# Moving the low halves of seven x tiles 128 bytes further on in SBUF: an attention and two MLPs on one Trainium2 core

## The chip, the core and the metric

The kernel runs on one core of one Trainium2 chip. The metric is the device time of one execution in microseconds, measured from outside the core's first and last instruction. A profiled execution has a time of its own, a span (first to last instruction) and a trace of every engine.

## What is computed

A causal block attention is followed by two MLPs, all in float32:

```python
scores = scale * np.matmul(q, k.transpose(0, 1, 3, 2))       # q, k, v: 4 x 8 x 576 x 64
scores = np.where(block_i >= block_j, scores, -1e9)          # blocks of 64
attn = softmax(scores)
x = (attn @ v) as 2304 x 512
h = x @ w_in;  x = (h * np.cos(h)) @ w_out                   # d_model 512, d_ff 2048
h = x @ w2_in; x = (np.maximum(h, 0) ** 2) @ w2_out
```

## The kernel before

**Parts and halves.** Each float32 operand of a large product is split into a high half (rounded to float32r) and a low half (the rest). A product is then three matmuls, written by `mm3` (L903): weights high with x high, weights high with x low, weights low with x high. In a matmul the `lhsT` operand is loaded into the array as weights by an instruction of its own, and the `rhs` operand, here x, streams through. Each matmul of the program reloads its weights, so while one matmul streams x, the weights of the next are being loaded.

**Stages.** In the first part (to about 405 us of the span) attention runs on all engines, interleaved with half of the first MLP; nothing of it is touched by the change. From there to the end, three stages run (L1537 on, `R.phase` 5 to 7): the other half of the first MLP, the first half of the second MLP, and its second half. Each stage takes the tokens in five chunks (`ROUNDS`): four of 512 tokens, one of 256. For each chunk there are two `quad` calls (`two` for the chunk of 256), c = 0 and c = 1. A `quad` (L1366) is a Strassen-Winograd product of 2 by 2 blocks: seven products, each of one of seven weight forms with one of seven x forms. One product (L1345) is 12 matmuls of 128 x 128 weights with 256 columns: two column halves m, two row halves k, three matmuls of `mm3`. All are recorded at L548 and named `h<-x,w` in the profile; there are 2304. Products onto `y` (the second matrix of each MLP) run between and among them.

**The order** is set by a list scheduler in the file (`Recorder`), which works on costs of its own and knows no addresses. Each engine then executes its instructions in that order.

**Where the operands lie.** The seven x forms are tiles `x0` to `x6` (`x_tile`, L1299) of [128, 2, 2, 256] float32r: per partition 2048 bytes of high half, then 2048 bytes of low half. They are written by `x_parts` (L1302), and in the second stage also copied to DRAM (`xp_d<-x`); the third stage loads them from there (`x<-xp_d`, `kept_parts`, L1316). The weight forms of c = 0 lie in the pool `wo`, those of c = 1 in the pool `wa` (`factors`, L773), each [128, 2, 512] with the low half 2048 bytes behind the high one. In the built program the starts of these tiles within a partition, modulo 512 bytes, are:

| tiles | start modulo 512 |
|---|---|
| x0 to x6, high and low halves alike | 320 |
| weights of c = 0 (pool `wo`), high and low | 384 |
| weights of c = 1 (pool `wa`), high and low | 256 |
| g tiles (second operand of the y products of the first two stages) | 64 |

All steps from one k, m or half to the next are multiples of 512 bytes. This text calls *distance* the start of the streamed operand less the start of the weights that are loaded meanwhile (the next matmul's), modulo 512 bytes. In a run of products of one `quad` it is the same at every matmul: 448 for c = 0, 64 for c = 1.

Of the kernel before, what the change touches and what calls it, by code (L numbers as in the profile page):

```python
# [2 lines left out]

# [8 lines left out]
F32R = mybir.dt.float32r  # L12
# [6 lines left out]
PSUM = bass.MemoryType.PSUM  # L19
# [37 lines left out]
class View:  # L57
    def __init__(self, vt, chain, ix, halves):
        self.vt, self.chain, self.ix, self.halves = vt, chain, ix, halves
# [34 lines left out]


class VTile(View):
    def __init__(self, pool, shape, dtype, tag, bufs, whole=False):
        self.pool, self.shape, self.dtype, self.tag, self.bufs = pool, shape, dtype, tag, bufs
        self.whole = whole
        n = int(np.prod(shape[1:]))  # L100
        self.grain = 32 if n >= 32 else 1
        self.full = (1 << (2 * (n // self.grain + 1))) - 1
        self.real = None
        self.users = []
        self.bank = self.banks = self.before = None
        super().__init__(self, [], np.arange(n).reshape(shape[1:]), 3)

    def alloc(self):
        if self.real is None:
            tag = self.tag if self.bank is None else f"bank{self.bank}"  # L110
            self.real = self.pool().tile(self.shape, self.dtype, tag=tag, name=self.tag, bufs=self.bufs)


class Banks:
# [30 lines left out]
class Recorder:  # L145
# [20 lines left out]
        self.kind = None  # L166
        self.phase = 0

    def tile(self, pool, shape, dtype, tag, bufs=1, whole=False):
        return VTile(pool, shape, dtype, tag, bufs, whole)  # L170

    @contextmanager
    def of(self, kind):
# [199 lines left out]
def f(v):  # L373
    return v.bitcast(F32)


def real(v):
    return v.ap() if isinstance(v, View) else v
# [3 lines left out]
def kernel(  # L382
# [25 lines left out]
    R = Recorder()  # L408


    def of(kind):
        def wrap(fn):
            def run(*args, **kw):
                with R.of(kind):
                    return fn(*args, **kw)

            return run

        return wrap
# [40 lines left out]
    def hi_part(hi, x):  # L460
        n = hi.size
        flexible(
            "hi",
            {
                "POOL": (
                    "POOL", n * 0.836 + 160,
                    lambda: nc.gpsimd.tensor_scalar(real(hi), real(x), 1.0, 1.0, op0=ALU.mult, op1=ALU.mult),  # L467
                ),
                "DVE": (
                    "DVE", n / 1.92 + 68, lambda: nc.vector.tensor_scalar(real(hi), real(x), 1.0, None, op0=ALU.mult), 2,  # L470
                ),
                "ACT": ("ACT", n / 1.2 + 92, lambda: nc.scalar.activation(real(hi), real(x), ACTF.Copy)),  # L472
            },
            [hi], [x],
        )

    def lo_part(lo, x, hi):
        n = lo.size
        if psum(x):
            return tt(lo, x, f(hi), ALU.subtract)  # L480
        flexible(
            "lo",
            {
                "POOL": (
                    "POOL", n * 2.1 + 350,
                    lambda: nc.gpsimd.tensor_tensor(real(lo), real(x), real(f(hi)), op=ALU.subtract), 1,
                ),
                "DVE": (
                    "DVE", n / 0.96 + 68,
                    lambda: nc.vector.tensor_tensor(real(lo), real(x), real(f(hi)), op=ALU.subtract), 1,  # L490
                ),
            },
            [lo], [x, hi],
        )
# [76 lines left out]
    def dma(out, in_, size, service=None):  # L571
        R.op(
            "DMA", max(400.0, size / 360.0), lambda: nc.sync.dma_start(out=real(out), in_=real(in_)), [out], [in_],
            lat=1250,
        ).service = size / 420.0 if service is None else service
# [5 lines left out]
    class Pool:  # L581


        def __init__(self, name, **kw):
            self.name, self.kw, self.pool, self.after, self.stack = name, kw, None, (), None
# [18 lines left out]
    def later(names, **kw):  # L604
        return [Pool(n, **kw) for n in names]
# [32 lines left out]
    xs_p, tmp = opened(s1, "xs1", "tmp1")  # L638
    (sb,) = opened(att, "att", side="right")

    def T(pool, shape, dtype, tag, bufs=1):
        return R.tile(pool, shape, dtype, tag, bufs, whole=pool.kw.get("space") == PSUM)

    x_d = T(dram, [KD, 128, NT], F32, "x_d")
    y1_d = T(dram, [KD, 128, NT], F32, "y1_d")
    y_d = T(dram, [KD, 128, NT], F32, "y_d")


# [27 lines left out]
    for i in range(2):  # L676
# [3 lines left out]
        whole = T(sb, [128, 128], F32, f"whole{i}")  # L680
# [585 lines left out]
    for group, steps in WORK:  # L1266
# [6 lines left out]
        if group in ((0, 2), (1, 1)):  # L1273
            c = group[0]
            left_weights(w1_in, 2 + c, wi_d[c])
        if group in ((1, 2), (2, 1)):
            c = group[0] - 1
            staged_weights(row_chunks(w1_out, 2 + c, 3 + c), wo_d[c:c + 1])
        if group == (3, 1):
            wo_p, x3_p = later(("wo", "x3"), side="right")  # L1280
# [9 lines left out]
    def raw_rows(src, c0, n):  # L1290
# [5 lines left out]
            raw.append(t)  # L1296
        return raw

    def x_tile(j):  # L1299
        return T(x3_p, [128, 2, 2, 256], F32R, f"x{j}")  # L1300

    def x_parts(forms, keep):  # L1302

        ops = {}
        for j, x in forms:
            t = x_tile(j)
            hi, lo = t[:, 0], t[:, 1]
            hi_part(hi, x)
            lo_part(lo, x, hi)
            if keep is not None:  # L1310
                dma(keep[j], f(t).rearrange("p j k c -> p (j k c)"), 524288)
            ops[j] = hi, lo
        return ops

    @of("forms")
    def kept_parts(keep, which):  # L1316

        ops = {}
        for j in which:
            t = x_tile(j)  # L1320
            dma(f(t).rearrange("p j k c -> p (j k c)"), keep[j], 524288)
            ops[j] = t[:, 0], t[:, 1]
        return ops

    @of("forms")
    def load_plain(src, c0, keep=None):

        x1, x2 = raw_rows(src, c0, 256)
        d = T(tmp3, [128, 2, 256], F32, "t0")
        add(d, x2, x1, ALU.subtract)  # L1330
        return x_parts(((0, x1), (1, x2), (4, d)), keep)

    @of("forms")
    def load_quarters(src, c0, keep=None):

        raw = raw_rows(src, c0, 512)
        b11, b12, b21, b22 = [t[:, :, o:o + 256] for t in raw for o in (0, 256)]
        t1, t2, t3, t4 = [T(tmp3, [128, 2, 256], F32, f"t{i}") for i in range(4)]
        add(t1, b12, b11, ALU.subtract)
        add(t2, b22, t1, ALU.subtract)  # L1340
        add(t3, b22, b12, ALU.subtract)
        add(t4, b21, t2, ALU.subtract)
        return x_parts(enumerate((b11, b21, b22, t4, t1, t2, t3)), keep)
# [193 lines left out]
    for stage in range(3):  # L1537
# [4 lines left out]
        for turn_, i in enumerate(ROUNDS[stage]):  # L1542
# [3 lines left out]
            if stage < 2:  # L1546
                xs = (load_quarters if i < 4 else load_plain)(src, c0, xp_d[i] if stage and turn_ < 4 else None)
                g = new_g()
            else:
                if turn_:  # L1550
                    xs = kept_parts(xp_d[i], FIRST if i < 4 else (0, 1, 4))
                g = g_forms()
# [27 lines left out]
            if stage < 2 and 0 < turn_ < 3:  # L1580
                c = 2 * stage + turn_ - 1
# [61 lines left out]
```

## Time and profile before

| what | value |
|---|---|
| median of 3 runs | 973.34 us (973.02 to 973.65) |
| time of the profiled execution | 974.84 us |
| its span | 973.0 us |
| mean granted TensorE clock | 0.994 of full speed |
| instructions | 19283 |
| TensorE busy (PE) | 98% of the span, 6996 matmuls |
| VectorE, ScalarE, GpSimd busy | 73%, 62%, 21% |
| HBM traffic | 189 GB/s over the span |

PE stands for TensorE's matmuls, PEld for its weight loads, which overlap them; DVE is VectorE, ACT ScalarE, POOL GpSimd, SP the queue that issues the transfers. Matmuls are pipelined: one lasts longer than the time to the start of the next. The time that a matmul costs is therefore read as the length of a stretch divided by the matmuls in it, called *pitch* below, and not as the mean duration of one.

### The profile page before, as it was taken

The page shows a single profiled execution, that of the slowest core. Times are in us where ns is not written, and L with a number is a line of the kernel's source. Part 1 is how long each engine was busy: PE and PEld are TensorE (multiplying, and loading weights), DVE is VectorE, ACT ScalarE, POOL GpSimd, SP SyncE. Part 2 cuts the span into 40 slices and gives each one's busy share as a digit, 9 for nine tenths or more (in the row PEclk, how much of TensorE's full clock was granted, in tenths as well). Part 3 has the DMA queues.
Part 4 walks back from the last instruction along what each step waited for, and adds up shares of the span by engine and source line. Part 5 has one row for each costly group of instructions (what it writes and reads, how often), then busy time and mean ns, then how long its engine had stood idle before and what let it go on. Part 6 is the DMA issues. An engine that isn't in the chain of part 4 may idle for free.

```text
span 973.0 us, 19283 instructions
## 1 busy us (share of the span) xinstructions
PE 951.8 (98%) x6996; PEld 856.1 (88%) x6996; DVE 713.8 (73%) x1581; ACT 602.3 (62%) x1285; POOL 208.3 (21%) x313
## 2 busy tenths in 40 slices
PE   7979999999999999999999999999999999999998
PEld 5757987889898989999989889998898899999998
DVE  5898667687877455588879797987885737659565
ACT  5787588785889575484758476767564433324222
POOL 3554243447687781000000000000000000000000
PEclk8999999999999999999999999999999999999999
DMA  6755233355656347563355899796947779535321
GB/s 184 192 150 124 67 85 84 105 153 182 176 174 206 109 134 263 200 254 93 109 173 181 317 360 327 268 352 215 358 139 240 245 256 416 194 104 195 96 73 60
DMA packets 155150, 185.29 MB, mean 190 GB/s; under 512 B 71728, under 2 KB 119856, under 8 KB 155056
## 3 DMA queue, kind: packets, MB, share of 16 engines
q1 hardware_dynamic: 155056, 184.07, 57.5%
q8 instruction: 55, 0.90, 0.4%
q14 instruction: 39, 0.32, 0.1%
HBM read 114.29 MB, written 69.73 MB: 189 GB/s over the span
## 4 chain that ended last, share of the span: by engine, by line
PE 88%; DMA 5%; DVE 3%; ACT 2%; issue 1%; POOL 1%; SPq 0%; ACTq 0%; POOLq 0%; DVEq 0%
PE y L548 37%; PE h L548 34%; PE t L566 6%; PE a L558 5%; PE s L558 4%; DMA wi_d<-so 2%; PE s L548 1%; DMA x<-xp_d 1%; DMA w<-wf_d 1%; DMA x<-x_d 1%; DVE e L1046 1%; POOL e L531 0%; DVE c L449 0%; DVE c L748 0%; DVE so L490 0%
## 5 line engine op out<-in xcount | busy, mean ns | idle before, releaser
L548 PE MATMUL h<-x,w 128*128 128x256 f32 x2304 | 315.8, 278 | 1.7 <-DVE r L442 0.9
L548 PEld LDWEIGHTS h<-x,w 128*128 128x128 f32 x2304 | 294.4, 188 | 6.5 <-DVE r L442 1.7
L548 PE MATMUL y<-gh,w 128*128 128x256 f32 (+2 forms) x832 | 214.7, 329 | 7.3 <-POOL w L467 6.6
L548 PEld LDWEIGHTS y<-gh,w 128*128 128x128 f32 x832 | 144.3, 189 | 19.0 <-POOL w L467 7.6
L548 PE MATMUL y<-gl,w 128*128 128x256 f32 (+2 forms) x416 | 135.0, 328 | 0.0
L548 PE MATMUL y<-w,gh 128*128 128x512 f32 (+1 forms) x450 | 124.0, 354 | 0.4 <-DVE gh L490 0.4
L548 PEld LDWEIGHTS y<-w,gh 128*128 128x128 f32 x450 | 78.9, 188 | 12.6 <-DVE gh L490 0.6
L433 ACT ACTIVATE e<-e,st 128x256 f32<-128x256 f32 (+4 forms) x144 | 82.9, 577 | 8.6 <-DVE st L1046 6.9
L1046 DVE CUSTOM_DVE_ANT_0 e<-s,mask 128x128 f32<-128x128 f32 (+4 forms) x160 | 71.3, 478 | 22.9 <-PE s L558 15.3
L531 POOL TENSOR_SCALAR e<-e,st 128x256 f32<-128x256 f32 (+4 forms) x116 | 73.0, 640 | 63.0 <-DVE st L1067 37.0
L548 PEld LDWEIGHTS y<-gl,w 128*128 128x128 f32 x416 | 78.5, 189 | 6.2 <-issue 0.8
L548 PE MATMUL y<-w,gl 128*128 128x256 f32 (+1 forms) x306 | 83.5, 333 | 0.0
L472 ACT ACTIVATE gh<-r 128x512 fp32r<-128x512 f32 (+1 forms) x85 | 51.3, 610 | 40.0 <-DVE r L1404 18.2
L566 PE MATMUL t<-ident,e 128*128 128x128 f32 (+1 forms) x400 | 65.1, 282 | 4.6 <-DVE e L535 2.3
L490 DVE TENSOR_TENSOR gl<-r,gh 128x512 fp32r<-128x512 f32 (+1 forms) x83 | 54.7, 664 | 15.3 <-ACT gh L472 12.4
L442 DVE TENSOR_TENSOR o<-y,o 128x512 f32<-128x512 f32 (+1 forms) x55 | 34.8, 635 | 40.2 <-PE y L548 39.1
L548 PE MATMUL h<-xs2h,w 128*128 128x320 f32 x256 | 62.0, 313 | 0.0
L566 PEld LDWEIGHTS t<-ident,e 128*128 128x128 f32 (+1 forms) x400 | 46.4, 141 | 13.8 <-POOL e L531 4.7
L501 ACT ACTIVATE r<-t 128x384 f32<-128x384 f32 (+1 forms) x95 | 49.2, 531 | 14.6 <-PE t L566 13.1
L433 ACT ACTIVATE t<-raw,minus 128x512 int32<-128x512 int8 x64 | 48.8, 762 | 14.8 <-DMA raw<-in_moe_w_out_dram 6.8
L548 PEld LDWEIGHTS y<-w,gl 128*128 128x128 f32 x306 | 50.2, 188 | 6.1
L548 PE MATMUL h<-xs1h,w 128*128 128x256 f32 x256 | 53.5, 290 | 1.2 <-POOL w L467 0.7
(172 smaller groups left out, 1838.0 us busy)
## 6 DMA issues: line engine op xcount, KB each, us to landing
wi_d<-so SPq DMA_DIRECT2D x84, 256.0 KB, 2.8
w<-wi_d SPq DMA_DIRECT2D x42, 512.0 KB, 6.3
raw<-in_moe_w_in_dram SPq DMA_DIRECT2D x32, 512.0 KB, 4.6
raw<-in_moe_w_out_dram SPq DMA_DIRECT2D x32, 512.0 KB, 4.4
xp_d<-x SPq DMA_DIRECT2D x24, 512.0 KB, 6.0
x<-xp_d SPq DMA_DIRECT2D x24, 512.0 KB, 5.7
y_d<-o SPq DMA_DIRECT2D x34, 256.0 KB, 2.6
o<-y_d SPq DMA_DIRECT2D x32, 256.0 KB, 3.8
```

Source lines behind the costliest of these rows:

```text
L433: return nc.scalar.activation(real(out), real(in_), func, **kw)
L442: out.size / 0.96 + 68, lambda: nc.vector.tensor_tensor(real(out), real(a), real(b), op=op), [out], [a, b],
L472: "ACT": ("ACT", n / 1.2 + 92, lambda: nc.scalar.activation(real(hi), real(x), ACTF.Copy)),
L490: lambda: nc.vector.tensor_tensor(real(lo), real(x), real(f(hi)), op=ALU.subtract), 1,
L501: "ACT": ("ACT", n / 1.2 + 50, lambda: nc.scalar.activation(real(out), real(ps), ACTF.Copy)),
L531: lambda: nc.gpsimd.tensor_scalar(real(out), real(x), real(s), 1.0, op0=ALU.mult, op1=ALU.mult),
L548: lambda: nc.tensor.matmul(real(ps), lhsT=real(lhsT), rhs=real(rhs), start=start, stop=stop, skip_group_check=True),
L558: nc.tensor.matmul(real(ps), lhsT=real(l), rhs=real(r), start=start, stop=stop, skip_group_check=True)
L566: lambda: nc.tensor.transpose(real(out), real(in_), real(ident)[0:rows, 0:rows]), [out], [in_, ident],
L1046: lambda: nc.vector.tensor_tensor_reduce(out=real(e), in0=real(ps), in1=real(m), scale=-1.0, scalar=BIG, op0=ALU.add, op1=ALU.min, accum_o ...
```

## The change

The x tiles get 32 float32 elements (128 bytes) between their high and their low half, and as many behind: `x_tile` asks for `apart=32`, `VTile.alloc` allocates [128, 1024 + 32] and builds the view with a step of 512 + 32 elements between the halves. The transfers to and from `xp_d` are written as two pieces of 2048 bytes per partition, where they were one of 4096. Nothing else is edited, and the instructions of all engines stand in the same order as before.

```diff
     def alloc(self):
...
+            if not self.apart:
+                self.real = self.pool().tile(self.shape, self.dtype, tag=tag, name=self.tag, bufs=self.bufs)
+                return
+
+            n, m = int(np.prod(self.shape[1:])), int(np.prod(self.shape[2:]))
+            t = self.pool().tile([self.shape[0], n + self.apart], self.dtype, tag=tag, name=self.tag, bufs=self.bufs)
+            a = t[:, 0:n].rearrange("p (a b c) -> p a b c", a=self.shape[1], b=self.shape[2])
+            self.real = dataclasses.replace(a, ap=[a.ap[0], [m + self.apart, self.shape[1]], *a.ap[2:]])
...
     def x_tile(j):
-        return T(x3_p, [128, 2, 2, 256], F32R, f"x{j}")
+        return T(x3_p, [128, 2, 2, 256], F32R, f"x{j}", 1, 32)
...
-                dma(keep[j], f(t).rearrange("p j k c -> p (j k c)"), 524288)
+                dma(by_half(keep[j]), f(t).rearrange("p j k c -> p j (k c)"), 524288)
...
-            dma(f(t).rearrange("p j k c -> p (j k c)"), keep[j], 524288)
+            dma(f(t).rearrange("p j k c -> p j (k c)"), by_half(keep[j]), 524288)
```

In the built program the starts modulo 512 become (the weights and g tiles stay where they were; the two `x` buffers of the same pool, which hold raw rows and later two weight forms of the third stage, move by 896 bytes, from 320 to 448):

| tile | high half | low half |
|---|---|---|
| x0, x5 | 448 | 64 |
| x1, x6 | 64 | 192 |
| x2, x3 | 192 | 320 |
| x4 | 320 | 448 |

The distances of a product alternate in the pattern d, d + 128, d over the three matmuls of `mm3`. For c = 0, d is 64, 192, 320 or 448 by the tile's row of the table; for c = 1 it is 128 more.

## Rows read from the trace of the kernel before

**Rows 1.** The page's busy times by engine: busy us, share of the span, instructions.
```profile
PE 951.8 (98%) x6996; PEld 856.1 (88%) x6996; DVE 713.8 (73%) x1581; ACT 602.3 (62%) x1285; POOL 208.3 (21%) x313
```

**Rows 2.** The page's chain that ended last: shares by engine, then by line.
```profile
PE 88%; DMA 5%; DVE 3%; ACT 2%; issue 1%; POOL 1%; SPq 0%; ACTq 0%; POOLq 0%; DVEq 0%
PE y L548 37%; PE h L548 34%; PE t L566 6%; PE a L558 5%; PE s L558 4%; DMA wi_d<-so 2%; PE s L548 1%; DMA x<-xp_d 1%; DMA w<-wf_d 1%; DMA x<-x_d 1%; DVE e L1046 1%; POOL e L531 0%; DVE c L449 0%; DVE c L748 0%; DVE so L490 0%
```

**Rows 3.** PE's waits, 405 to 973 us: total us, times, longest.
```profile
PE h L548 <- DVE r L442: 0.9, 2, 0.6
...
PE h L548 <- DMA x<-xp_d: 0.2, 1, 0.2
```

**Rows 4.** The chain in order of time: start us, us, engine line, matmuls.
```profile
511.40 2.83 PE h L548 x24
...
616.93 4.24 PE h L548 x36
...
639.16 5.00 PE h L548 x43
...
706.71 15.01 PE h L548 x132
...
837.59 10.88 PE h L548 x96
...
953.53 5.42 PE h L548 x46
```

**Rows 5.** Groups of PE by shape in 639.0-641.8, then 642.3-644.1 us: busy us, mean ns.
```profile
L548 PE MATMUL h<-x,w 128*128 128x256 f32 x24 | 3.0, 279 | 0.0
...
L548 PE MATMUL h<-x,w 128*128 128x256 f32 x17 | 2.1, 276 | 0.0
```

**Rows 6.** PE's timeline at 594.1 and at 597.5 us: start us, us, operation.
```profile
594.05 0.28 PE L548 MATMUL h<-x,w 128*128 128x256 f32 x1
594.17 0.28 PE L548 MATMUL y<-gh,w 128*128 128x256 f32 x1
594.29 0.28 PE L548 MATMUL h<-x,w 128*128 128x256 f32 x1
...
597.49 0.28 PE L548 MATMUL h<-x,w 128*128 128x256 f32 x1
597.60 0.28 PE L548 MATMUL y<-gl,w 128*128 128x256 f32 x1
597.71 0.28 PE L548 MATMUL h<-x,w 128*128 128x256 f32 x1
```

**Rows 7.** The chain again, two stretches of y at one distance each.
```profile
372.57 7.54 PE y L548 x64
...
891.40 1.91 PE y L548 x16
```

**Rows 8.** Groups of PE by shape, 405 to 973 us: busy us, mean ns, idle before.
```profile
L548 PE MATMUL h<-x,w 128*128 128x256 f32 x2304 | 315.8, 278 | 1.7 <-DVE r L442 0.9 <-ACT p L501 0.4 <-DMA x<-xp_d 0.2
...
L548 PE MATMUL y<-x,gl 128*128 128x256 f32 x54 | 8.7, 282 | 0.0
```

**Rows 9.** The chain's pieces that are a transfer: start us, us.
```profile
422.01 7.49 DMA x<-x_d
...
553.48 7.83 DMA wi_d<-so
...
811.42 10.21 DMA x<-xp_d
```

**Rows 10.** DMA issues: KB each, median us to landing.
```profile
wi_d<-so SPq DMA_DIRECT2D x84, 256.0 KB, 2.8
...
xp_d<-x SPq DMA_DIRECT2D x24, 512.0 KB, 6.0
x<-xp_d SPq DMA_DIRECT2D x24, 512.0 KB, 5.7
...
x<-x_d SPq DMA_DIRECT2D x8, 512.0 KB, 5.7
```

More of the change, by code (lines that the diff above doesn't have):

```diff
@@ L1 @@
+import dataclasses
 import heapq
@@ L96, with __init__ @@
 class VTile(View):
-    def __init__(self, pool, shape, dtype, tag, bufs, whole=False):
+    def __init__(self, pool, shape, dtype, tag, bufs, whole=False, apart=0):
         self.pool, self.shape, self.dtype, self.tag, self.bufs = pool, shape, dtype, tag, bufs
-        self.whole = whole
+        self.whole, self.apart = whole, apart
         n = int(np.prod(shape[1:]))
@@ L110, in alloc @@
             tag = self.tag if self.bank is None else f"bank{self.bank}"
-            self.real = self.pool().tile(self.shape, self.dtype, tag=tag, name=self.tag, bufs=self.bufs)
+            if not self.apart:
[5 more added lines that the diff above has]
+            self.real = dataclasses.replace(a, ap=[a.ap[0], [m + self.apart, self.shape[1]], *a.ap[2:]])
 class Banks:
@@ L167, in __init__, with tile @@
         self.phase = 0
-    def tile(self, pool, shape, dtype, tag, bufs=1, whole=False):
-        return VTile(pool, shape, dtype, tag, bufs, whole)
+    def tile(self, pool, shape, dtype, tag, bufs=1, whole=False, apart=0):
+        return VTile(pool, shape, dtype, tag, bufs, whole, apart)
     @contextmanager
@@ L639, with T @@
     (sb,) = opened(att, "att", side="right")
-    def T(pool, shape, dtype, tag, bufs=1):
-        return R.tile(pool, shape, dtype, tag, bufs, whole=pool.kw.get("space") == PSUM)
+    def T(pool, shape, dtype, tag, bufs=1, apart=0):
+        return R.tile(pool, shape, dtype, tag, bufs, pool.kw.get("space") == PSUM, apart)
     x_d = T(dram, [KD, 128, NT], F32, "x_d")
@@ L1297, in raw_rows, with by_half @@
         return raw
+    def by_half(t):
+        return t.rearrange("p (j c) -> p j c", j=2)
     def x_tile(j):
-        return T(x3_p, [128, 2, 2, 256], F32R, f"x{j}")
+        return T(x3_p, [128, 2, 2, 256], F32R, f"x{j}", 1, 32)
     def x_parts(forms, keep):
```

## The prediction

> **What bounds the kernel now.** I read the busy times first: TensorE's matmuls fill 98% of the span [rows 1]. The chain of waits says the same, 88% of it PE, 34% at the `h` products, with 5% transfers [rows 2]. Then PE's waits from 405 us to the end, the only part that the change touches: two of 0.9 us together [rows 3] and five more of 0.4 us or less, some 2.5 us in 568. So from 405 us on the time is the number of matmuls times their pitch, apart from a few stretches in which the chain runs through transfers and PE's speed counts for nothing.
>
> Next I divided stretches of the chain by their matmuls [rows 4]. All are the same instruction, 256 columns, at the full clock, yet there are two paces. 36 matmuls from 616.93 take 4.24 us, 117.8 ns each, as do 24 from 511.40 (117.9) and 46 from 953.53 (117.8). But 96 from 837.59 take 10.88 us, **113.3 ns** each, and 132 from 706.71 take 15.01 (113.7). The step is 4.4 ns. It shows in the duration of one, too: 279 ns in the slow pace, 276 in the fast [rows 5]. The paces are not mixed matmul by matmul: a stretch has one of them and keeps it, through changes of tile and product.
>
> What ends a slow stretch? The stretch of 43 from 639.16 holds both [rows 4, 5]: its mean lies between, 116.3; up to 641.8 the duration is 279, from 642.3 it is 276. In between, the last product of one chunk (c = 1, distance 64) is followed by the first of the next (c = 0, distance 448), with no wait. Five other slow stretches that meet a change of distance between 448 and 64 without a pause end there in the same way, one of them only at a second change. In the other direction nothing happens: the 96 from 837.59 go from c = 0 to c = 1 after a quarter of them and stay at 113.3. And where h and y matmuls of 256 columns take turns, so that the distance alternates (64 at the h, 192 at the y) at each instruction, starts are 0.11 us apart at 597.5 [rows 6], and this pace holds for some 150 matmuls, up to 613; the alternation had begun at the slow pace, at 594.1 starts are still 0.12 apart [rows 6], and took about 2 us to leave it. So the fast pace survives any change among 64, 192, 320 and 448 that the trace has, and the slow one needs a constant distance. In the attention part, where all distances are constant, 64 y matmuls take 7.54 us, 117.8 each [rows 7]. That is how I read the rows; that a change of distance is the cause, and not what else changes with it, is inference.
>
> **The change, part by part.**
>
> *Low halves 128 bytes further on.* Of three matmuls of a product, the second now has another distance, so two of three transitions change it. By the above a slow stretch should end within a few matmuls of its begin, and a fast one should not notice. The price: each matmul moved from the slow to the fast pace gives 117.8 - 113.3 = 4.4 ns. I summed, over the 19 pieces of h in the chain that hold slow matmuls (five of them in rows 4), the time less 113.3 ns for each matmul: 0.11 for the one at 511.40, 0.16 at 616.93, 0.13 at 639.16, 0.05 at 706.71, 0.21 at 953.53, the other fourteen 0.02 to 0.13 each; together **1.6 us**. Three more slow stretches lie where the chain is a transfer, beside those at 422, 553 to 569 and 802 to 821 us [rows 9]; their 0.4 us are hidden by a wait that then grows by as much. A stretch takes some matmuls to change pace (about 10% to 20% of its length, as at 639.16), which leaves 1.4 us.
>
> *y products with an x buffer as streamed operand.* The third stage keeps two weight forms in the two raw buffers that move by 896 bytes. Their 108 matmuls (54 `y<-x,gl`, mean 282 ns [rows 8], and as many beside them) run at 1.91 / 16 = 119.4 ns [rows 7], at distance 0 or 256, the worst pace of the trace. Theirs becomes 128 or 384. Bounds: 113.3 would give 108 x 6.1 ns = 0.66 us, the present pace 0. I take 0.1, since a move by a multiple of 128 leaves the operands equally aligned to 128 bytes. h and y matmuls that take turns in the third stage have such distances too, some 225 h; a change of 1 ns either way is 0.2 us, and I take 0.
>
> *Transfers in two pieces per partition.* 24 `xp_d<-x` and 24 `x<-xp_d`, in 2048 byte pieces. The nearest row is `x<-x_d`, which writes the raw buffers in such pieces: 512 KB land in 5.7 us, as `x<-xp_d` did in one piece; the writes have a neighbour in `wi_d<-so`, 1024 byte pieces, 2.8 us for half the size against 6.0 [rows 10]. So 0. From above: only the first seven loads at 811.42 are waited for, 0.2 us by PE [rows 3, 9]; a tenth more on their 10.21 us would cost 1 us. What is queued behind them on SP are loads for later products. Issue order and engine work are unchanged: 0.
>
> **The sum.** 974.84 us of the profiled execution less 1.4 and 0.1 is 973.3. That execution stands 1.50 us above the median of the runs, so on their scale it is 973.34 - 1.5 = **971.8 us**, -0.15%. A measurement of this kernel tells about 0.2%, 1.95 us, from no change; the forecast lies inside.
>
> **The rivals.**
>
> *Addresses have no part in it.* The pace could be an accident of when a stretch begins, redrawn by any new layout. For it: slow stretches begin after pauses, and 64 and 448 occur at both paces. Against it: rows 7, where distance 0 or 256 always goes with 119.4. The same share slow gives no change, 973.3 us; the draw could shift it by 1 us either way. By the Trainium skill (TensorE: Matmul & The Clock Gate, Part 2, step 1) TensorE has two independent read ports of SBUF, and loading the next weights takes no read bandwidth from the running matmul, so that the change would be worth nothing, 973.3. The trace does not agree: the same instruction has 113.3 and 119.4 ns, by the operands' places.
>
> *The slow pace becomes the rule.* This one ends slower than before. Distances 320 and 192, which h products did not have after 405 us, could be the ones that hold it, or a change within a product could be answered by a delay each time. For it: in the attention part the distance is 320 and nearly all is slow [rows 7]. Then some 1900 h matmuls that are fast now would each pay 4.4 ns, 8 us, of which about 85% lie on the chain: 973.3 + 7 = 980 us. It decides as soon as a quarter of the fast ones turn slow (1900 x 0.25 x 4.4 ns = 2.1 us). Against it: alternation with 192 [rows 6] at the fast pace.
>
> *More than the h stretches.* If the y matmuls above and the alternating ones of the third stage also reach 113.3, 0.7 + 0.8 us come on top: 970.3.
>
> **How the numbers follow.** Forecast 0.57, no part 0.20, slow rule 0.15, more 0.08. The range reaches from the last rival, 970.3, to 975.0: the middle rival's shift, and a slow pace that wins in part. Faster by over 0.2% (below 971.4): a third of the forecast, all of the last rival, some of the second, 0.30. Slower (above 975.3): 0.15 and a little of the second, 0.17. The rest, 0.53, is the same.
>
> **What would show it.** Right: h pieces of the chain at 113.3 to 114 throughout, mean duration 276 rather than 278 in the group of 2304, its busy time about 2 us lower; y groups as they were; part before 405 us unchanged; the wait of h on `x<-xp_d` grown by 0.1 to 0.2 us. Wrong: stretches of h at 117.8 with the new alternation, or a third pace between; then a change of distance does not end the slow pace. If h is fast throughout and the time still is not lower, the gain has gone into the waits beside the transfers [rows 9].

## The result: slower by 0.66%, and the profile after

The changed kernel takes 980.20 us (median of 6 runs, 977.87 to 981.97); the kernel before 973.33 beside it. The ratio is 1.0066, with an interval of 1.0052 to 1.0080. The profiled execution took 980.25 us with a span of 978.4, so 5.4 us of span came on top.

The page's busy times, the chain by engine and by line, the group of h products, and two of the transfers' issue lines, of the kernel after:

```profile
PE 957.6 (98%) x6996; PEld 862.7 (88%) x6996; DVE 713.8 (73%) x1581; ACT 602.6 (62%) x1285; POOL 208.8 (21%) x313
...
PE 89%; DMA 4%; DVE 3%; ACT 2%; POOL 1%; issue 1%; SPq 0%; POOLq 0%; DVEq 0%; ACTq 0%
...
L556 PE MATMUL h<-x,w 128*128 128x256 f32 x2304 | 321.3, 280 | 1.0 <-DVE r L450 0.6
...
xp_d<-x SPq DMA_DIRECT2D x24, 512.0 KB, 6.6
x<-xp_d SPq DMA_DIRECT2D x24, 512.0 KB, 6.7
```

Against [rows 1, 2, 8, 10]: PE and its weight loads are busy for longer, by 5.8 and 6.6 us, and no other engine by more than 0.5. The h products went from 315.8 to 321.3 us and from 278 to 280 ns each. The transfers to and from `xp_d` land 0.6 and 1.0 us later, but less of the chain runs through transfers (4% for 5%). PE's waits from 405 us on, which answer to [rows 3], total 1.8 us:

```profile
PE h L556 <- DVE r L450: 0.6, 1, 0.6
PE h L556 <- DMA x<-xp_d: 0.4, 1, 0.4
PE y L556 <- DVE gh L498: 0.4, 1, 0.4
PE y L556 <- ACT gh L480: 0.4, 1, 0.4
```

So no wait took the time (before, the waits of this part total 2.5 us). Nor did the clock: from 405 us on the granted clock is 1.00 of full speed in both traces. The chain's pieces of h, in order of time (start us, us, matmuls), which answer to [rows 4]:

```profile
512.86 2.84 PE h L556 x24
...
619.64 4.24 PE h L556 x36
...
642.13 5.07 PE h L556 x43
...
710.24 15.50 PE h L556 x132
...
841.66 11.27 PE h L556 x96
...
958.96 5.42 PE h L556 x46
```

The stretches that were slow before are as they were: 4.24 us for 36, 5.42 for 46. The stretches at the short pitch have the long one now: 132 take 15.50 us for 15.01, **117.4 ns** each for 113.7; 96 take 11.27 for 10.88, 117.4 for 113.3. Over all h matmuls after 405 us, the mean time from one start to the next matmul's start, called *spacing* below, rose from 114.97 to 117.57 ns (the few that wait are left out). If each is averaged with its neighbours, six at a time, 1402 of these averages lie below 114.8 ns before, and none after. 2304 x 2.6 ns is 6.0 us. The y matmuls of 256 columns rose by 0.5 ns (0.4 us together), those of 512 by 0.3 (0.2 us). Together this is 6.6 us; the medians differ by 6.9. The part before 405 us, which the change does not touch, has the same PE time in both traces (389.4 and 389.7 us).

So the second rival of the prediction, the slow pace as the rule, happened, and the experiments ask what in the change does it.

### The profile page after: what moved, and what is told of

Same layout as the page of the kernel before. It is cut to its first block, busy times and chain, and to the rows that moved or that the text cites. A ratio compares the mean times of both kernels' runs of the same rounds, so it can differ in the third digit from the quotient of the medians.

```text
span 978.4 us, 19283 instructions
## 1 busy us (share of the span) xinstructions
PE 957.6 (98%) x6996; PEld 862.7 (88%) x6996; DVE 713.8 (73%) x1581; ACT 602.6 (62%) x1285; POOL 208.8 (21%) x313
## 4 chain that ended last, share of the span: by engine, by line
PE 89%; DMA 4%; DVE 3%; ACT 2%; POOL 1%; issue 1%; SPq 0%; POOLq 0%; DVEq 0%; ACTq 0%
PE y L556 37%; PE h L556 36%; PE t L574 6%; PE a L566 5%; PE s L566 4%; DMA wi_d<-so 2%; PE s L556 1%; DMA x<-xp_d 1%; DMA w<-wf_d 1%; DVE e L1054 1%; DMA w<-wi_d 1%; POOL e L539 0%; DVE c L457 0%; DVE c L756 0%; SPq L581 0%
## 5 line engine op out<-in xcount | busy, mean ns | idle before, releaser
L556 PE MATMUL h<-x,w 128*128 128x256 f32 x2304 | 321.3, 280 | 1.0 <-DVE r L450 0.6
L556 PEld LDWEIGHTS h<-x,w 128*128 128x128 f32 x2304 | 299.8, 188 | 5.2 <-DVE r L450 1.1
```

Of the source, the lines that this page charges most:

```text
L556: lambda: nc.tensor.matmul(real(ps), lhsT=real(lhsT), rhs=real(rhs), start=start, stop=stop, skip_group_check=True),
```

## The experiments

The theories:

- **Theory 1**: x's own start. Consecutive matmuls that stream from starts that differ modulo 256 bytes are, or become, slow.
- **Theory 2**: any alternation of the distance between streamed start and weights.
- **Theory 3**: an x that starts at 192 modulo 256 (before, all started at 64) is slow by itself.
- **Theory 4**: the transfers in two pieces.
- **Theory 5**, which came up on the way: a change of the distance, but only one that x makes.

The first four look back to one fact that the prediction had passed over: before the change every x and every g began at 64 modulo 256, so the changes of distance in [rows 4 to 6] all came from the weights' side. "Mean spacing" below is that of h matmuls after 405 us, as above (114.97 ns before, 117.57 after), and each is read from the one profiled execution of its kernel. The kernel before, run beside the three groups of experiments, took 973.89 (the first four), 973.39 (the next four) and 973.84 us (the last two). The diffs show the lines that matter; those with `1, 32` on their minus side, and the one of the tiles 128 bytes apart, edit the changed kernel.

### A gap of 256 bytes

```diff
-        return T(x3_p, [128, 2, 2, 256], F32R, f"x{j}", 1, 32)
+        return T(x3_p, [128, 2, 2, 256], F32R, f"x{j}", 1, 0 if j in (2, 3) else 64)
```

> The gap between the halves is 256 bytes in x0, x1, x4, x5, x6 and none in x2, x3: the distance still alternates (by 256) within ten of fourteen products, but every x half starts at 64 modulo 256, as before the change. Theory 1 (the slow pace is kept up by a change of the streamed operand's own start modulo 256 from one matmul to the next): as before the change, 972 to 974 us, long chain pieces of h back at 113 to 114 ns, mean duration of an h matmul 276 to 279. Theory 2 (any alternation of the distance keeps it up): five of seven products slow, about 978 us, pieces at 117 to 118. Theory 3 (an x operand that starts at 192 modulo 256 is slow by itself): 973. Theory 4 (the transfers in two pieces): 980.

Measured: 975.22 us, ratio 1.0014 (1.0002 to 1.0026), mean spacing 114.90 ns. The group of h and two pieces of the chain:

```profile
L556 PE MATMUL h<-x,w 128*128 128x256 f32 x2304 | 315.2, 278 | 2.1 <-DVE r L450 1.1
```

```profile
707.25 15.10 PE h L556 x132
...
837.94 10.88 PE h L556 x96
```

114.4 and 113.3 ns each: the fast pace is back although the distance alternates in five of seven x forms. Theory 2 falls. The time is 0.14% up all the same, above theory 1's 972 to 974 us and just clear of its interval; the trace shows nothing for it (h has the spacing of before, y of 256 columns too, with 116.9 ns), so this remainder stays unexplained.

### Tiles 128 bytes apart, halves together

```diff
-            self.real = dataclasses.replace(a, ap=[a.ap[0], [m + self.apart, self.shape[1]], *a.ap[2:]])
+            self.real = dataclasses.replace(a, ap=[a.ap[0], [m, self.shape[1]], *a.ap[2:]])
```

> 128 bytes lie behind each x tile and none between its halves: the starts modulo 256 differ from tile to tile (four tiles at 192, three at 64) and are constant within a product. Theory 1: the start changes only between products, once in 12 matmuls, so 972 to 975 us and most pieces of h at 113 to 114 ns. Theory 2: the distance is constant within a product, 972 to 975. Theory 3: the products of the tiles at 192 run at 117.7 ns, four in seven, about 977 us. Theory 4: 980.

Measured: 978.04 us, ratio 1.0039 (1.0024 to 1.0054), mean spacing 116.98 ns. Theory 1 had this too fast, and theory 3 had the time right for another reason: products at 64 are slow as well. A stretch of seven consecutive products of c = 0, x0, x1, x5, x4, x6, x2, x3, each by its own window of the timeline (start us, us from the first start to the last end):

```profile
750.59 1.57 PE L556 MATMUL h<-x,w 128*128 128x256 f32 x12
...
752.00 1.53 PE L556 MATMUL h<-x,w 128*128 128x256 f32 x12
...
753.37 1.57 PE L556 MATMUL h<-x,w 128*128 128x256 f32 x12
...
754.78 1.53 PE L556 MATMUL h<-x,w 128*128 128x256 f32 x12
...
756.14 1.52 PE L556 MATMUL h<-x,w 128*128 128x256 f32 x12
...
757.50 1.57 PE L556 MATMUL h<-x,w 128*128 128x256 f32 x12
...
758.92 1.58 PE L556 MATMUL h<-x,w 128*128 128x256 f32 x12
```

x0, x5, x2 and x3 start at 192, x1, x4 and x6 at 64. Each switch between them switches the pace: 1.57 us for 12 is the slow one, 1.52 to 1.53 the fast. The way back from slow takes three matmuls: the spacings of x1 begin 117, 116, 114, then 113.

Here this looks like theory 3, but in c = 1, whose weights start 128 bytes elsewhere modulo 256, it is the other way round: x at 64 runs at 117.9 ns, x at 192 at 115.8. I sorted the pairs of products of one c that follow directly on each other, each with at least six matmuls in a row, by what x's start did, with the pace taken from the last six matmuls of each:

| from one product to the next | pairs | slow afterwards |
|---|---|---|
| x moves by 128, to a distance of 64 modulo 256 | 33 | 33 |
| x moves by 128, to a distance of 192 modulo 256 | 31 | 11 |
| x does not move | 23 | 19, each of which was slow before |

A move towards 64 always ends in the slow pace, a move towards 192 mostly in the fast one, and without a move the pace stays what it is. **Within one c of this run, the pace is set where the streamed start moves, and kept where nothing moves.** This is theory 1, sharpened. A move of x changes the distance too, which this run can't tell apart; the runs that move the weights do. In the change, each product moves between 64 and 192 at two of three matmuls, so every second move goes towards 64, and three matmuls for the way back are never there; that this is why it stays slow is inferred.

### The transfers alone

```diff
-        return T(x3_p, [128, 2, 2, 256], F32R, f"x{j}", 1, 32)
+        return T(x3_p, [128, 2, 2, 256], F32R, f"x{j}", 1, 0)
```

> Only the transfers to and from xp_d are written in two pieces; the tiles lie as before the change. Theories 1 to 3: 973 us, within 0.2% of the kernel before, pieces of h at 113 to 114 ns. Theory 4: 979 to 981.

Measured: 974.89 us, ratio 1.0001 (0.9990 to 1.0013), mean spacing 115.08 ns. Its issue lines:

```profile
xp_d<-x SPq DMA_DIRECT2D x24, 512.0 KB, 5.7
x<-xp_d SPq DMA_DIRECT2D x24, 512.0 KB, 5.9
```

Two pieces cost nothing that this can tell, and the 6.6 and 6.7 us of the kernel after are not theirs. Theory 4 falls.

### The weights' low halves moved for x's

```diff
-            ts_ = {i: w_tile(pool, n) for i in ORDERS[turn]}
+            ts_ = {i: w_tile(pool, n, 32 if n == 7 else 0) for i in ORDERS[turn]}
```

The x tiles have no gap here, `w_tile` hands the gap on to the tile, and `shim4` grows so that x stays at 64. The gap also lies behind each weight tile, so from tile to tile whole weight forms differ by 128 bytes too.

> The low halves of the c = 0 weights begin 128 bytes further on, and x stays as before (all halves at 64 modulo 256). The distance changes over the three matmuls of a step exactly as in the change, but by the weights' place. Theory 1: no slower than before, 970 to 974 us, c = 0 products at 113 to 114 ns. Theory 2: half the h products (c = 0) at 117.7 ns, about 976 to 977 us. Theory 3: 973. Theory 4: 973.

Measured: 976.23 us, ratio 1.0022 (1.0011 to 1.0032), mean spacing 115.39 ns. The group and one piece of the chain:

```profile
L556 PE MATMUL h<-x,w 128*128 128x256 f32 x2304 | 316.6, 278 | 0.7 <-DVE r L450 0.6
```

```profile
836.37 10.97 PE h L556 x96
```

The same alternation of the distance, by the weights' place, leaves 96 at 114.3 ns. The kernel is 0.2% slower all the same: 0.4 ns on 2304 h is 1.0 us, and the y matmuls of 256 columns went from 116.95 to 117.43 ns, another 0.4. That is 1.4 of the 2.3 us. So theory 1's "no slower" was a little too good, and theory 2 falls here too (it wants 117.7 ns in c = 0; the mean there is 115.7, for 115.2 before).

This trace also tests the prediction's own step, with the weights in x's place. The first two products of a stretch of c = 0, each by its own window of the timeline:

```profile
747.63 1.57 PE L556 MATMUL h<-x,w 128*128 128x256 f32 x12
...
749.04 1.52 PE L556 MATMUL h<-x,w 128*128 128x256 f32 x12
```

The first begins slow, the second is fast. Take all stretches of c = 0 with at least 22 h matmuls in a row, and call one slow where six spacings average over 115.5 ns: 11 of 16 begin slow here, and 10 of these 11 are fast at their end, after 3 to 17 matmuls. In the kernel before 5 of 16 begin slow and 1 of the 5 ends fast (the 24 from 511.40 in [rows 4] stay slow). No fast one turns slow. So an alternation that the weights make does end the slow pace and leaves the fast one alone, as the prediction said; the mean is no lower because more stretches begin slow.

### Both moved together

In c = 0, x0, x1 and x4 now keep one distance within a product while their own start alternates; x5, x6, x2 and x3 have a constant start and an alternating distance.

```diff
-        return T(x3_p, [128, 2, 2, 256], F32R, f"x{j}")
+        return T(x3_p, [128, 2, 2, 256], F32R, f"x{j}", 1, 32 if j in (0, 1, 4) else 0)
...
-            ts_ = {i: w_tile(pool, n) for i in ORDERS[turn]}
+            ts_ = {i: w_tile(pool, n, 32 if n == 7 else 0) for i in ORDERS[turn]}
```

> x0, x1 and x4 have the gap of 128 bytes, the other x tiles none, and the low halves of the c = 0 weights are moved by 128 bytes as well. In c = 0 the products of x0, x1 and x4 then keep one distance while x's own start alternates. Theory 1, sharpened by the run of the padded tiles (a change of x's own start modulo 256 starts the slow pace, which then stays until something ends it): x0, x1 and x4 at 117 to 118 ns in c = 0 and c = 1 alike, the others what they inherit, 977 to 979 us. Theory 5 (it is a change of the distance, but only one made by x): x0, x1 and x4 at 113 to 114 ns in c = 0, slow in c = 1; about 976 us.

Measured: 981.00 us, ratio 1.0081 (1.0060 to 1.0101), mean spacing 117.39 ns. The same seven products of c = 0 as above, in the order x0, x1, x5, x4, x6, x2, x3, by their windows of the timeline:

```profile
753.12 1.61 PE L557 MATMUL h<-x,w 128*128 128x256 f32 x12
...
754.56 1.61 PE L557 MATMUL h<-x,w 128*128 128x256 f32 x12
...
756.01 1.53 PE L557 MATMUL h<-x,w 128*128 128x256 f32 x12
...
757.38 1.57 PE L557 MATMUL h<-x,w 128*128 128x256 f32 x12
...
758.79 1.53 PE L557 MATMUL h<-x,w 128*128 128x256 f32 x12
...
760.15 1.59 PE L557 MATMUL h<-x,w 128*128 128x256 f32 x12
...
761.58 1.59 PE L557 MATMUL h<-x,w 128*128 128x256 f32 x12
```

The first two and the fourth, x0, x1 and x4, are slow at a constant distance (over all c = 0: 118.4, 118.8 and 117.7 ns; in c = 1: 117.5, 117.7 and 117.3). In the stretch shown, that distance is 192 modulo 256 at x0 and x1 (1.61 us, slower than the 1.57 of the slow pace) and 64 at x4, so no one value of it makes the slowness. x5 and x6 get back to 113 ns at an alternating distance. So a move of x's own start is slow without any change of the distance. Theory 5 falls. x2 and x3 have a constant start and are slow here; both are entered by a move of x by 128, which fits the table above but is not a separate proof. That gaps in three tiles of seven make the whole as slow as the change was not expected (977 to 979).

### All x moved by 128 bytes

```diff
-                    shim(stack, "shim4", 64, side="right")
+                    shim(stack, "shim4", 192, side="right")
```

> All x tiles are moved by 128 bytes together, no gap: every x starts at 192 modulo 256, and x's start changes only between h and y matmuls (g stays at 64). Theory 1, sharpened: no change within h; a run of h that is entered towards a distance of 64 modulo 256 (c = 0) begins slow and stays so, one towards 192 (c = 1) is mostly fast: c = 0 at 117 to 118 ns, c = 1 at 113 to 115, 973 to 976 us. Theory 3 (192 is slow by itself): all h at 117.7 ns, 980 us.

Measured: 977.53 us, ratio 1.0046 (1.0028 to 1.0063), mean spacing 116.57 ns.

```profile
L548 PE MATMUL h<-x,w 128*128 128x256 f32 x2304 | 319.0, 279 | 0.5 <-DVE r L442 0.4
```

```profile
708.19 15.45 PE h L548 x132
...
838.97 11.32 PE h L548 x96
```

The direction is theory 1's: x's start moves only between y and h, and c = 0 (distance 64) is slow. Counted are products that follow directly on a y matmul and have at least six matmuls in a row, by the mean of their last six spacings: all 21 of c = 0 are slow (4 of 21 in the kernel before). c = 1 is mixed, 16 of 23 slow (14 of 23 before), where "mostly fast" was expected, and the time is above the 973 to 976 forecast. Theory 3 falls: 581 of the averages over six lie below 114.8 ns, all at a start of 192.

### Two other places

Weights of c = 1 moved by 128 bytes as a whole, x as before (their pool `wa` also holds operands of y, 918 streamed and 522 loaded as weights after 405 us, and weights of the first part; they move along):

```diff
+    shim(ctx, "shim5", 128)
     (wa_p,) = opened(ctx, "wa")
+    shim(ctx, "shim6", 128)
```

> x stays as before; the weights of c = 1 (pool wa) are moved by 128 bytes as a whole, so that c = 0 and c = 1 have the same distance of 192 modulo 256, which in the runs so far held the slow pace less often than 64. Theory 1: no slower than before, 970 to 973 us, h at 113 to 115 ns in both c. Theory 3: 973. If the distance plays no part in what ends the slow pace: 973 and c = 1 unchanged at 114.7 ns.

Measured: 977.74 us, ratio 1.0044 (1.0023 to 1.0065), mean spacing 116.19 ns. All x at 192 and the weights of c = 0 moved by 128:

```diff
-                if i:
-                    shim(stack, "shim4", 64, side="right")
+                if i or len(opens) > 1:
+                    shim(stack, f"shim4{i}", 64 if i else 128, side="right")
```

> All x at 192 modulo 256 and the weights of c = 0 moved by 128 bytes, so that both c have a distance of 192, and each run of h after y begins with a change of the streamed start by 128. Theory 1, sharpened: h mostly at 113 to 115 ns, while y matmuls that stream g (at 64) are entered towards a distance of 64 and begin slow: h gains up to 3 us, y of the first stage loses up to 2 us, 971 to 975 us. Theory 3: 980.

Measured: 977.64 us, ratio 1.0044 (1.0030 to 1.0058), mean spacing 115.80 ns. Pieces of the two chains, first of the one with the weights moved, then of the other:

```profile
709.68 15.55 PE h L548 x132
...
839.92 11.32 PE h L548 x96
```

```profile
709.24 15.55 PE h L548 x132
...
840.38 10.91 PE h L548 x96
```

Both expectations failed: a distance of 192 everywhere does not keep h fast. Long stretches begin slow after y and stay so: counted as above, 25 of 44 products behind a y matmul are slow in the first and 26 of 44 in the second, 18 of 44 in the kernel before. The same 132 matmuls are slow in both, the same 96 slow in one and fast in the other. What sets the pace of a stretch at its entry from y is thus not the distance of h alone, and the rule from the padded tiles is not enough to choose a layout. In the first run y itself is slower too: its matmuls of 256 columns have a mean spacing of 118.0 ns for 116.95.

The two runs do show what the weights' place is worth inside h. Where products of one c follow directly on products of the other that have the slow pace, with three matmuls or more before and five or more behind, both have the same distance here, and all 26 such places stay slow. In the kernel before the distance goes from 64 to 192 modulo 256 from c = 1 to c = 0 with x at rest, and all four such places turn fast, as the prediction had read.

### y operands at one place

The right factors of the third stage that lie in `raw`, `x` and `so` are moved to 0 modulo 256; nothing of h is moved. (The last argument is the first element that a tile uses in its buffer; `ROOM` lists the tags whose buffers are made larger for it.)

```diff
-                    t = T(pool, [128, 2, 2, 256], F32R, tag, n)
+                    t = T(pool, [128, 2, 2, 256], F32R, tag, n, 48 if tag in ROOM else 0)
```

> The kernel before, with another thing moved: those right factors of the third stage that lie in the buffers raw, x and so and are streamed by 270 of the y matmuls begin 192 bytes further on, at 0 modulo 256 as the other streamed factors in pool wa, where they began at 64 or 192; their stationary operands all begin at 64. In the kernel before, y matmuls whose streamed start and next weights' start differ by 0 or 128 modulo 256 had a mean distance of 118 to 120 ns between starts in every product, the others 114 to 115. If that and the number of changes of the streamed start set the pace, these y products go to 114 to 116 ns, which is about 1 us: 971.5 to 973 us, faster than both kernels. If the place plays no part for y: 973.3.

Measured: 973.76 us, ratio 0.9996 (0.9985 to 1.0006). Groups of y from 800 us to the end, first of the kernel before, then of this one:

```profile
L548 PE MATMUL y<-w,gh 128*128 128x256 f32 x162 | 32.1, 281 | 0.4 <-DVE gh L490 0.4
...
L548 PE MATMUL y<-raw,gh 128*128 128x256 f32 x54 | 8.4, 281 | 0.0
...
L548 PE MATMUL y<-raw,ws 128*128 128x256 f32 x54 | 7.9, 282 | 0.0
```

```profile
L555 PE MATMUL y<-w,gh 128*128 128x256 f32 x162 | 32.2, 282 | 0.5 <-DVE gh L497 0.4
...
L555 PE MATMUL y<-raw,gh 128*128 128x256 f32 x54 | 8.2, 278 | 0.0
...
L555 PE MATMUL y<-raw,ws 128*128 128x256 f32 x54 | 7.7, 278 | 0.0
```

The 270 moved ones did nearly what was expected: their mean spacing goes from 118.9 to 116.0 ns. But the 480 that were not moved went from 116.5 to 117.3, and h from 800 us on from 115.4 to 115.6. What is left is 0.2 us, where 1 was forecast. No kernel of this study beats the kernel before by more than its interval.

### A gap of 64 bytes

```diff
-        return T(x3_p, [128, 2, 2, 256], F32R, f"x{j}", 1, 32)
+        return T(x3_p, [128, 2, 2, 256], F32R, f"x{j}", 1, 16)
```

> The change with a gap of 64 bytes for one of 128: x starts at 0, 64, 128 and 192 modulo 256, and the streamed start still changes at two of three matmuls. Theory 1 (any change of x's own start modulo 256 that the step of 128 bytes stands for): h at 117 to 118 ns, 979 to 982 us. If only a change by half of 256 bytes starts the slow pace: h nearer to 115 ns and 973 to 976 us.

Measured: 981.29 us, ratio 1.0066 (1.0049 to 1.0083), mean spacing 118.45 ns, the highest of all. The same two stretches:

```profile
711.59 15.71 PE h L556 x132
...
843.09 11.46 PE h L556 x96
```

119.0 and 119.4 ns. A step of 64 bytes is no better than one of 128; of the steps tried only 256 is harmless.

### All kernels beside each other

| what moves | mean spacing of h, ns | ratio to the kernel before |
|---|---|---|
| nothing (before) | 114.97 | 1 |
| gap of 256 bytes | 114.90 | 1.0014 |
| y operands of the third stage | 115.06 | 0.9996 |
| transfers in two pieces | 115.08 | 1.0001 |
| low halves of c = 0 weights | 115.39 | 1.0022 |
| all x, and c = 0 weights | 115.80 | 1.0044 |
| c = 1 weights | 116.19 | 1.0044 |
| all x | 116.57 | 1.0046 |
| x tiles 128 bytes apart | 116.98 | 1.0039 |
| gaps in three x, and c = 0 weights | 117.39 | 1.0081 |
| the change, gap of 128 bytes | 117.57 | 1.0066 |
| gap of 64 bytes | 118.45 | 1.0066 |

Each ns on the 2304 h matmuls is 2.3 us, 0.24%. The ratios rise with that to within 0.25%, not in strict order; y's pace, which is not in the table, and the intervals leave room for the rest, which is not worked out here. In all these kernels PE executes the same instructions in the same order.

## Why the prediction was wrong

**What bounds the kernel** was right: after the change as before, the time from 405 us on is the number of matmuls times their pitch, and what the change moved is how many of h's matmuls have the slow one of the two paces.

**The step that failed** is the sentence "a slow stretch should end within a few matmuls of its begin, and a fast one should not notice". Its ground was that the fast pace "survives any change among 64, 192, 320 and 448 that the trace has". In that trace those changes came through the weights, or went between x and g, which both start at 64 modulo 256. The change moves x itself. Where the weights make the alternation, the sentence holds within a stretch: 10 of 11 slow stretches end, and no fast one turns slow. Made by x it fails in both halves: the slow stretches did not end (4.24 and 5.42 us as before), and no fast one is left (1402 averages below 114.8 ns, then none). The distance alone was the wrong quantity: at a constant one x0, x1 and x4 are slow, and at an alternating one, made by the weights or by steps of 256 bytes, fast stretches stay fast. So the term of -1.6 us on the chain became a loss. Summed over all of the chain's h pieces, the time above 113.3 ns for each matmul rose from 3.9 us (1929 matmuls) to 9.4 (2033), +5.5, beside the span's difference of 5.4.

**The y products with an x buffer** (-0.1 us) stayed at 281 ns for 282: no gain to speak of, as the small term said.

**The transfers** (0) were right as a price: alone they give 1.0001. Nothing of the upper bound of 1 us shows; PE waited 0.4 us on `x<-xp_d` for 0.2.

**The rivals.** "The slow pace becomes the rule" was worked out at 980 us and happened at 980.2; with 0.15 it was held too unlikely. That the time fits so closely is in part luck: the rival took some 1900 h matmuls as fast, where by the averages over six 1402 were, and left out the y matmuls, which added 0.6 us. Its reason, "a change within a product could be answered by a delay each time", is near to what the runs show; the argument set against it, the fast alternation in [rows 6], is the same confusion of x's changes with the weights'. "Addresses have no part in it" falls with the rows of the table from 1.0039 up: beside transfers that cost nothing, only places differ there, and they shift the median by 4.1 to 7.6 us, where this rival allowed 1. By the Trainium skill (TensorE: Matmul & The Clock Gate, Part 2, step 1) the two read ports are independent; by that all these layouts would take 973 us. The runs do not agree: 0.9996 to 1.0081 of it was measured.

**What stays open.** What in the chip makes the two paces isn't shown by any run. Also open is why stretches that begin after y get the pace they get: the two layouts with one distance for both c had more slow entries than the kernel before, and no rule found here foretells that.

## What to carry to other kernels

Where TensorE is busy throughout, the same instruction in the same order can take 113 or 118 ns by where its operands start: read the pitch as a stretch of the chain divided by its matmuls, before and after any change that moves a tile, one that seems only to pad or to shift a pool included. In this kernel, operands that are streamed one after another are best kept at the same start modulo 256 bytes, so pad by multiples of 256. That alone is not enough: the three layouts in which x never moves within h, but x or the weights lie elsewhere, cost 0.44 to 0.46%. And before a pattern in a trace is used as a law, list what never varied in it: here the streamed start.

## What was not expected of the hardware

- The pace of matmuls of 256 columns is kept: in the run of the padded tiles 23 of 23 pairs of products without a move of x kept it, 33 of 33 moves by 128 bytes towards a distance of 64 ended slow, and the way from slow to fast took three matmuls (117, 116, 114, then 113 ns).
- The weights' place has a part in it too: alternating by 128 bytes, the weights end 10 of 11 slow stretches, where the kernel before ends 1 of 5.
- The start modulo 256 bytes matters for the streamed operand: gaps of 64 and 128 bytes give 118.45 and 117.57 ns, one of 256 gives 114.90. The same alternation made by the weights gives 115.39.
- Moving whole pools by 128 bytes, with no change inside a product, costs 0.44 to 0.46% of this kernel's time.
